# The projection of the token batches in two nested levels of seven products

## The chip, the cores and the metric

The kernel runs on one core of a Trainium2 chip. The metric is the time of one execution on the device in microseconds; before the change it is 779.3 us, the median of three runs (778.61 to 779.39).

## What is computed

Eight batches of 512 tokens (8 heads of 64) attend to 32 state rows for each head, and the state rows attend to the tokens. The two results, 8 x (512 + 32) = 4352 rows of 512 numbers, then go through a gated feed-forward layer, all in float32:

```python
scores = scale * np.matmul(x, state.transpose(0, 1, 3, 2))     # softmax over the state -> a
xread = np.matmul(a, state)
scores2 = scale * np.matmul(state, x.transpose(0, 1, 3, 2))    # softmax over the tokens -> a2
sread = np.matmul(a2, x)
attn = np.concatenate([xread, sread], axis=2)
# (batch, rows, heads * 64) -> x: 4352 x 512
xn = x / np.sqrt(np.mean(x * x, axis=-1, keepdims=True) + 1e-6) * rms_g
g = xn @ w_gate                                                # 512 x 1536
out = (g * (1.0 / (1.0 + np.exp(-g))) * (xn @ w_val)) @ w_out  # 1536 x 512
```

## The kernel before, in words

A batch of tokens has three kinds of work. Its *attention* (`tokens_read`, `states_read`) gives softmax weights `aT_s` and the state rows' results. Its *hidden* part (`hidden_seven`) gives `hb`, 1536 hidden channels by 512 tokens, held as 12 blocks of 128 channels. Its *projection* (`project_seven`) multiplies `hb` by `w_out`, held as `wo` in SBUF. The weights for the hidden part are first multiplied by the batch's own state rows (`own_weights`, L548, two blocks of 128 channels at a time), from `w_m`, which is fetched from DRAM for each batch in six pieces of 1 MB (`fetch`, L169). The state rows of all batches come last, as a stage of their own with half as many columns.

Hidden part and projection use the same trick: a product of two matrices, each cut into 2 x 2 blocks, is made from seven block products instead of eight, with sums of blocks before and after (Winograd's form of Strassen's method). In the projection, `hb` is cut into halves of its channels and of its tokens, `wo` into halves of its channels and of its columns. Each of the seven products of a batch is 2 x 6 matmuls with 128 x 128 stationary and 128 x 256 moving numbers. The sums of `wo` (`weight_sums`, three in `wt`, one in place of a block of `wo`) are made once; the sums of `hb` (`hs`, L908) are made by VectorE in each batch. Products that belong to more than one result accumulate in one PSUM bank: ScalarE copies a bank out (L893) before the next product is added to it, and VectorE adds other banks to the copies (L901), which are then stored (L923). There are two PSUM banks `fx` and one each of `fy` and `fz` for these sums, in the hidden part and in the projection alike.

In the hidden part of batches 1 to 7, VectorE adds the banks (L756), ScalarE takes tanh of half of the gate channels (L747), VectorE makes the gate from it (L759) and multiplies by the values (L771). L775 and L781 are two more sums of halves that the projection needs. GpSimd makes the sums of the own weights (L574 to L577) and of the softmax weights (`slot_sums`, L612 to L615).

For batches 2 to 7, tokens are transposed in 32 x 32 blocks by VectorE (L310), written to DRAM (`x_d`, L313) and read back (`xG`, L318) so that L328 can multiply them by the state; softmax weights go the same way (`e_d`, L475 and L479). These transfers are issued by ScalarE, all others by SyncE (SP). `x` of a batch comes as 16 transfers (L114) into one of two buffers.

The order of instructions on TensorE, VectorE and ScalarE is written out by hand as strings, one letter for one step of a stream: `ORDER` for batch 0 with the conversion of the weights, `PERIOD` for each of batches 1 to 7, `STATES` for the state rows. In `PERIOD`, `h`, `t`, `u` are products, copies and sums of the hidden part, `p`, `c`, `k` those of the projection, `v` and `x` products and copies of the own weights, and `a`, `s`, `w` the attention and first own weights of the next batch. GpSimd's and SP's instructions are not bound by the strings; the framework places them.

```python
    by_hand = dict(engines={mybir.EngineType.PE, mybir.EngineType.DVE,
                            mybir.EngineType.Activation})
...
        with tc.manual_schedule(**by_hand):
            for stream in PERIOD:
                if stream in streams:
                    step = next(streams[stream], done)
```

## Time and profile before

| quantity | value |
|---|---|
| median of three runs | 779.3 us |
| span of the profiled execution | 776.3 us |
| period of one batch, 2 to 6 | 83.48 us |
| TensorE busy in such a period | 83.5 us |
| VectorE, ScalarE, GpSimd busy in it | 57.3, 31.1, 21.7 us |
| data moved in it | 140 GB/s |
| states' hidden part (L694, 128 columns) | 717.94 to 753.67 us |
| granted TensorE clock | 1.000 |

The span runs from the first to the last instruction of one profiled execution; the median lies 3.0 us above it, and what lies around the span is not in the profile. A batch's period is the distance between the starts of its L328 matmuls. Busy time of TensorE is modelled by the profile: weight loads (PEld) overlap matmuls, and a float32 matmul appears as two instructions. A group's idle time is the time for which its engine stood still just before it.

### The profile page before, as it was taken

To read this page: it belongs to the slowest core of one execution; us is meant where nothing else is said; L and a number is where in the kernel's file an instruction comes from. 1 tells how busy PE (TensorE), PEld (TensorE's weight loads), DVE (VectorE), ACT (ScalarE), POOL (GpSimd) and SP (SyncE) were. 2 spreads that over 40 slices of the span, in tenths; PEclk is the share of its full clock that TensorE was granted. 3 is DMA by queue.
4 is the path that set the end of the run, shared out by engine and by line. 5 is a ranking of instruction groups with operands and counts; after the bars stand their busy time and mean duration, and the time that the engine had idled before them with its cause. 6 is when DMAs were issued, how large, how long until landed. Compare 5 with 4: busy or idle time off the path is not lost.

```text
span 776.3 us, 12116 instructions
## 1 busy us (share of the span) xinstructions
PE 764.7 (98%) x4726; PEld 586.1 (75%) x4726; DVE 538.0 (69%) x846; ACT 328.0 (42%) x538; POOL 162.8 (21%) x232
## 2 busy tenths in 40 slices
PE   6999999999999999999999999999999999999998
PEld 5643444788878887878878877888778878888996
DVE  4999988678647872888368764787378735881461
ACT  6798874554145222543245314532354314510320
POOL 2000004430053105320433015400621044300000
PEclk9999999999999999999999999999999999999999
DMA  9977845770266225630565036612543154100311
GB/s 291 258 261 284 320 148 159 200 260 4 92 196 255 59 72 184 237 109 35 160 211 196 1 102 223 243 34 69 204 163 109 42 174 165 55 14 27 124 55 28
DMA packets 73689, 113.00 MB, mean 146 GB/s; under 512 B 40864, under 2 KB 51616, under 8 KB 66720
## 3 DMA queue, kind: packets, MB, share of 16 engines
q1 hardware_dynamic: 60512, 92.75, 35.5%
q10 hardware_dynamic: 13120, 19.47, 8.5%
q8 instruction: 38, 0.62, 0.3%
q14 instruction: 19, 0.16, 0.1%
HBM read 87.56 MB, written 24.64 MB: 145 GB/s over the span
## 4 chain that ended last, share of the span: by engine, by line
PE 96%; DVE 2%; DMA 0%; POOL 0%; ACT 0%; issue 0%; SPq 0%
PE f L694 38%; PE f L856 36%; PE f L796 5%; PE pv L590 5%; PE at L548 3%; PE pv L548 3%; PE at L328 1%; PE at L490 1%; PE at L421 1%; PE at L300 1%; PE at L278 1%; DMA rows<-in_state_dram 0%; DVE raw L245 0%; DVE w_m L254 0%; DVE ex L249 0%; POOL ri L271 0%
## 5 line engine op out<-in xcount | busy, mean ns | idle before, releaser
L856 PE MATMUL f<-wo,hb 128*128 128x256 f32 x540 | 123.0, 382 | 0.0
L694 PE MATMUL f<-aT_s,v 128*128 128x256 f32 x504 | 119.7, 382 | 0.0
L856 PEld LDWEIGHTS f<-wo,hb 128*128 128x128 f32 x540 | 101.4, 190 | 23.2 <-issue 5.0
L694 PEld LDWEIGHTS f<-aT_s,v 128*128 128x128 f32 x504 | 93.5, 190 | 25.0 <-DVE c L756 5.9
L756 DVE TENSOR_TENSOR g<-g,f 128x512 f32<-128x512 f32 (+1 forms) x96 | 61.3, 650 | 68.3 <-PE f L694 40.3
L694 PE MATMUL f<-aT_t,vs 128*128 128x256 f32 x336 | 87.0, 381 | 0.0
L747 ACT ACTIVATE hb<-g 128x1024 f32<-128x1024 f32 (+1 forms) x48 | 48.3, 1005 | 87.6 <-DVE g L756 87.6
L271 POOL TENSOR_TENSOR ri<-ss,mhalf 128x4 f32<-128x4 f32 x8 | 9.1, 1132 | 349.6 <-DVE ss L375 233.5
L856 PE MATMUL f<-wt,hs 128*128 128x256 f32 x360 | 80.4, 379 | 0.0
L893 ACT COPY ot<-f 128x256 f32<-128x256 f32 x60 | 20.1, 371 | 134.7 <-PE f L856 134.7
L856 PEld LDWEIGHTS f<-wt,hs 128*128 128x128 f32 x360 | 68.2, 190 | 9.4 <-issue 0.2
L694 PEld LDWEIGHTS f<-aT_t,vs 128*128 128x128 f32 x336 | 63.2, 190 | 14.1 <-issue 5.0
L759 DVE SCALAR_TENSOR_TENSOR hb<-hb,g 128x1024 f32<-128x1024 f32 x42 | 53.8, 1281 | 13.1 <-ACT hb L747 13.1
L574 POOL TENSOR_TENSOR vs<-v 128x256 f32<-128x256 f32 x42 | 30.7, 731 | 137.5 <-ACT v L559 137.5
L559 ACT COPY v<-pv 128x512 f32<-128x512 f32 x42 | 22.7, 594 | 71.2 <-PE pv L548 71.2
L745 ACT COPY g<-f 128x512 f32<-128x512 f32 (+1 forms) x48 | 26.9, 560 | 56.3 <-PE f L694 56.3
L796 PE MATMUL f<-wo,hb 128*128 128x512 f32 x96 | 44.7, 598 | 0.0
L590 PE MATMUL pv<-aT_s,v 128*128 128x512 f32 x96 | 44.2, 597 | 0.0
L694 PE MATMUL f<-aT_s,vs 128*128 128x256 f32 x168 | 43.1, 379 | 0.0
L694 PE MATMUL f<-aT_t,v 128*128 128x256 f32 x168 | 43.1, 379 | 0.0
L856 PE MATMUL f<-wo,hs 128*128 128x256 f32 x180 | 41.5, 382 | 0.0
L856 PE MATMUL f<-wt,hb 128*128 128x256 f32 x180 | 40.8, 382 | 0.0
(142 smaller groups left out, 1245.0 us busy)
## 6 DMA issues: line engine op xcount, KB each, us to landing
w_m<-w_d SPq DMA_DIRECT2D x48, 1024.0 KB, 5.6
out_dram<-ot SPq DMA_DIRECT2D x56, 128.0 KB, 1.8
raw<-in_moe_w_val_dram SPq DMA_DIRECT2D x6, 1024.0 KB, 5.3
raw<-in_moe_w_out_dram SPq DMA_DIRECT2D x6, 1024.0 KB, 7.6
w_d<-w_m SPq DMA_DIRECT2D x6, 1024.0 KB, 4.9
x_b<-in_x_dram SPq DMA_DIRECT2D x96, 64.0 KB, 2.3
x_d<-xB ACTq DMA_DIRECT2D x6, 1024.0 KB, 4.3
xG<-x_d ACTq DMA_DIRECT2D x24, 256.0 KB, 5.0
```

What stands on the lines that cost most here:

```text
L548: TE.matmul(out=pv[e][Ns * j:Ns * j + Ns, :], lhsT=stT_g[b][D * e:D * e + D, j, :], rhs=w[D * e:D * e + D, j].rearrange("p m k f -> p (m k ...
L559: SE.copy(v[:, e].rearrange("p m k f -> p (m k f)"), pv[e])
L574: GE.tensor_tensor(out=vs[:, 0], in0=a21, in1=a22, op=ALU.add)
L590: TE.matmul(out=to[0], lhsT=lhs(i, k), rhs=r, start=(i == 0), stop=(i == len(rhs) - 1))
L694: TE.matmul(out=ps[:, i, 0:half], lhsT=l[:, i, :], rhs=r, start=(start and i == 0 and k == 0), stop=(k == len(lhs) - 1), skip_group_check= ...
L745: SE.copy(gates(q)[1], q["x"][:, :, 0:half])
L747: SE.activation(out=hb[:, 2 * mp:2 * mp + 2, 0:n].rearrange("p m (c t) -> p m c t", c=2), in_=q["g"][:, :, :, 0:half], func=ACTF.Silu if s ...
L756: VE.tensor_tensor(out=to, in0=to, in1=q[ps][:, :, 0:half], op=ALU.add)
L759: VE.scalar_tensor_tensor(out=h, in0=h, scalar=1.0, op0=ALU.add, op1=ALU.mult, in1=q["g"].rearrange("p m c t -> p m (c t)"))
L796: TE.matmul(out=banks[r], lhsT=hb[:, m, P * r:P * r + P], rhs=wo[:, m, :], start=(m == 0), stop=(m == NM - 1))
L856: TE.matmul(out=banks[name][:, r, :], lhsT=lhs(k)[:, P * r:P * r + P], rhs=rhs(k), start=(start and r == 0 and k == 0), stop=(k == HM - 1) ...
L893: SE.copy(to, banks[name][:, r, :])
```

## The change

In batches 1 to 7, the projection is done by `project_twice`: each of the seven products of half matrices is itself made from seven products of quarter blocks, so a batch has 49 products of 3 matmuls with 128 x 128 moving numbers. Batch 0 and the state rows are projected as before.

- The stationary side needs sums of quarters of `hb` or of its half sums: `quarter_sums`, four VectorE subtractions or additions of 384 elements a partition for each of the seven outer products, in two buffers.
- The moving side needs sums of quarters of `wo` and `wt`: `weight_quarters` makes them once, on GpSimd, during batch 1, three for each outer product, and writes them to DRAM; a fourth replaces a quarter in place. `fetch_quarters` reads the three (128 x 1152 numbers) for each outer product of each batch, into three buffers. `weights_back` undoes the sums in place, on GpSimd, ahead of the state rows.
- An outer product adds into two banks, of four and three quarters. ScalarE copies, VectorE adds banks, and `combine`, four GpSimd additions, makes the result from the seven quarters. The copies live in the two buffers that also hold `g` of the hidden part, and in one more.
- The gate of batches 1 to 7 is the activation function Silu itself instead of tanh with a VectorE step (L759 goes).
- `x` has one buffer after batch 0 and comes as four transfers of 256 KB; the token order that follows from this is put right by the store. `sS` has one buffer, `e2T` shares the one of `e2`.
- `PERIOD` is new, and the strings now also fix the order of GpSimd's and SP's instructions: fetches of weights (`f`), of quarter sums (`g`), loads (`l`) and stores (`o`) are streams of their own. In it L328 moves from the projection into the hidden part.

The diff, cut to its core:

```diff
-    "hhvthttxhauhhxhuauaahhtutaahtahvxvtuhuxxhuuhthtxuthuhtuhhuhuhhutuhutthuxuhxtxuhh"
-    "vhuuthhxthxtahuhathuuuxuuauthuthtahhuthuuuhuhpuuuhtuuucauapaaasaspkacpaspsspaaaa"
-    "aaaapkkcpccaakaaascuskaappkaaaaapssssaaaaksapkakasswwwxxpxkxxpccssx"
+    "vxqqhthtfhthhaxhhqqquuttuxahhhththhhuuuauutthqhaaaaGthutuvqqxxvxxqxhuhhqxutuhhtu"
+    "haukkthtvxqxxhhhhhuaaauutttkhhukqqqquuuathhhhhafaauutttsqauhhhhuthqqGuuusuqqqGgp"
+    "upauhqqfqstuuupgppukpppppaakplpfckkkkpqakaaqqgaakkqgkcppppppppppkakkkkoakkppapsc"
+    "cpkpcpggacakpsopakaappakpsakppksaaakkksppppppgkakakppakaakaookkakssppsosppcofasa"
+    "wwxxxssspcwxxxloof"
...
-        x_sb[b] = two.tile([P, NC, H * D], F32, name="x_b")
-        if b > 1:
-            for i in range(4 * NC):
-                c, g = divmod(i, 4)
-                nc.sync.dma_start(
-                    out=x_sb[b][Ns * g:Ns * g + Ns, c].rearrange("p (h d) -> p h d", h=H),
-                    in_=x[b, :, P * g + Ns * c:P * g + Ns * c + Ns, :].rearrange("h p d -> p h d"))
-            return
+        x_sb[b] = (one if b else x_0).tile([P, NC, H * D], F32, name="x_b")
...
-        sS = read[b] = two.tile([P, 2, NC, P], F32, name="sS")
+        sS = read[b] = (one if b else x_0).tile([P, 2, NC, P], F32, name="sS")
...
-        e2T = one.tile([P, 4, 2, NC, Ns], F32, name="e2T")
+        e2T = e2
...
+        if b == 1:
+            load_state(2)
+            load_x(2)
...
-            fetch(b * (NM // 2) + mp + W_BUFS)
+            if b == 0 or b == 1 and mp < 2:
+                fetch(b * (NM // 2) + mp + W_BUFS)
...
-        seven["pool"] = ctx.enter_context(tc.tile_pool(name="halves", bufs=7))
+        seven["w2"] = ctx.enter_context(tc.tile_pool(name="quarters_w", bufs=3))
+        seven["s2"] = ctx.enter_context(tc.tile_pool(name="quarters_h", bufs=2))
+        seven["k"] = ctx.enter_context(tc.tile_pool(name="kept", bufs=1))
...
+    def fetch_quarters(n):
+        if n < 7 * (B - 1):
+            w2_sb[n] = seven["w2"].tile([P, 3, QM, QD], F32, name="w2")
+            nc.sync.dma_start(out=w2_sb[n], in_=t2_d[n % 7])
+    def weight_quarters():
+        for o, (b11, b21, b12, b22) in enumerate(map(by_columns, outer_weights())):
+            w2 = seven["w2"].tile([P, 3, QM, QD], F32, name="w2")
+            for to, a, b in ((w2[:, 0], b12, b11), (w2[:, 1], b22, w2[:, 0]),
+                             (w2[:, 2], b21, w2[:, 1]), (b12, b22, b12)):
+                GE.tensor_tensor(out=to, in0=a, in1=b, op=ALU.subtract)
+                if to is b12:
+                    nc.sync.dma_start(out=t2_d[o], in_=w2)
+                yield
+    def by_columns(r):
+        return [r[:, QM * i:QM * i + QM, QD * j:QD * j + QD] for j in range(2) for i in range(2)]
...
+    def project_twice(b, store):
+        first = 7 * (b - 1)
+        hs = seven["s"]
+        def A(i, j):
+            return hb[:, HM * j:HM * j + HM, HS * i:HS * i + HS]
+        lefts = [A(0, 0), A(0, 1), A(0, 0), hs, A(1, 0), A(0, 1), A(1, 1)]
+        banks, inner, kept = {}, {}, {}
+        def bank(name, fresh):
+            if fresh:
+                pools = (fx, fx) if name == "x" else (fy, fz)
+                banks[name] = [pools[i].tile([P, 4 - i, QD], F32, name="f") for i in range(2)]
+            return banks[name]
+        def products():
+            rights = outer_weights()
+            for o in range(7):
+                name, fresh = "xyxzxzx"[o], o in (0, 1, 3)
+                to = bank(name, fresh)
+                (a11, a12, a21, a22), (b11, b21, b12, b22) = quarters(lefts[o]), by_columns(rights[o])
+                for n, (half, slot, lhs, rhs) in enumerate((
+                        (0, 0, a11, b11), (0, 2, a12, b21), (0, 3, a22, 2), (0, 1, 1, 1),
+                        (1, 2, 0, 0), (1, 1, 2, b12), (1, 0, 3, b22))):
+                    if isinstance(lhs, int):
+                        lhs = inner[o][:, lhs]
+                    if isinstance(rhs, int):
+                        rhs = w2_sb[first + o][:, rhs]
+                    for k in range(QM):
+                        TE.matmul(out=to[half][:, slot, :], lhsT=lhs[:, k, :], rhs=rhs[:, k, :],
+                                  start=(fresh and n in (0, 4) and k == 0), stop=(k == QM - 1),
+                                  skip_group_check=True)
+                    yield
+        def copies():
+            for what, name, pool in (("p1", "x", "g"), ("u2", "x", "g"), ("p5", "z", "k"), ("c21", "x", "g")):
+                k = kept[what] = (two if pool == "g" else seven["k"]).tile(
+                    [P, 8, QD], F32, name="kept", tag="g" if pool == "g" else "kept")
+                for i in range(2):
+                    SE.copy(k[:, 4 * i:4 * i + 4 - i], banks[name][i])
+                    if what == "c21" and i:
+                        combine(what, 1, 0)
+                    yield
+        ready = {}
+        def stores():
+            for what in ("p1", "p5", "u2", "c21"):
+                for r in range(2):
+                    store(*ready[what][r])
+                    yield
+        def combine(what, i, j):
+            k = kept[what]
+            ready[what] = []
+            GE.tensor_tensor(out=k[:, 1:3], in0=k[:, 0:1].to_broadcast([P, 2, QD]), in1=k[:, 1:3],
+                             op=ALU.add)
+            GE.tensor_tensor(out=k[:, 5:8:2], in0=k[:, 1:2].to_broadcast([P, 2, QD]),
+                             in1=k[:, 5:7], op=ALU.add)
+            GE.tensor_tensor(out=k[:, 1], in0=k[:, 5], in1=k[:, 6], op=ALU.add)
+            GE.tensor_tensor(out=k[:, 0:4:3], in0=k[:, 5:8:2], in1=k[:, 3:5], op=ALU.add)
+            for r in range(2):
+                at = 2 - 2 * r
+                ready[what].append((2 * i + r, HD * j, HD, k[:, at:at + 2].rearrange("p c f -> p (c f)")))
+        def add(what, name, i, j):
+            k = kept[what]
+            for n in range(2):
+                part = k[:, 4 * n:4 * n + 4 - n]
+                VE.tensor_tensor(out=part, in0=part, in1=banks[name][n], op=ALU.add)
+                if n:
+                    combine(what, i, j)
+                yield
+        def quarter_sums(o):
+            a11, a12, a21, a22 = quarters(lefts[o])
+            s = inner[o] = seven["s2"].tile([P, 4, QM, QD], F32, name="h2")
+            VE.tensor_tensor(out=s[:, 0], in0=a21, in1=a22, op=ALU.add)
+            yield
+            VE.tensor_tensor(out=s[:, 1], in0=s[:, 0], in1=a11, op=ALU.subtract)
+            yield
+            VE.tensor_tensor(out=s[:, 2], in0=a11, in1=a21, op=ALU.subtract)
+            yield
+            VE.tensor_tensor(out=s[:, 3], in0=a12, in1=s[:, 1], op=ALU.subtract)
+            yield
+        def half_sums(to, a, b):
+            for k in range(0, HM, QM):
+                VE.tensor_tensor(out=to[:, k:k + QM], in0=a[:, k:k + QM], in1=b[:, k:k + QM],
+                                 op=ALU.subtract)
+                yield
+        def sums():
+            yield from quarter_sums(0)
+            yield from quarter_sums(1)
+            yield from half_sums(A(0, 0), hs, A(0, 0))
+            yield from quarter_sums(2)
+            yield from add("p1", "y", 0, 0)
+            yield from half_sums(A(0, 1), A(0, 1), A(0, 0))
+            yield from quarter_sums(3)
+            yield from quarter_sums(4)
+            yield from quarter_sums(5)
+            yield from add("p5", "x", 1, 1)
+            yield from quarter_sums(6)
+            yield from add("u2", "z", 0, 1)
+        return products(), copies(), sums(), stores()
...
+            rows_ = out[T * b:T * b + S, c0:c0 + n]
+            if b < 2:
+                rows_ = rows_[P * r:P * r + P]
+            else:
+                rows_ = rows_.rearrange("(c g t) n -> g c t n", g=4, t=Ns)[r]
...
-                            mybir.EngineType.Activation})
+                            mybir.EngineType.Activation, mybir.EngineType.Pool,
+                            mybir.EngineType.SP})
...
-        h, t, u = hidden_seven(S, weights_of(b), lambda b=b: tokens_of(b), False)
-        p, c, k = project_seven(S, store_tokens(b))
...
+            h, t, u = hidden_seven(S, weights_of(b), lambda b=b: tokens_of(b), True)
+            p, c, k, o = project_twice(b, store_tokens(b))
+            streams.update(o=o, f=fetches(b), g=fetches_of_quarters(b))
+            if b == 1:
+                streams.update(q=weight_quarters(), G=first_fetches_of_quarters())
+            if b + 1 < B:
+                streams.update(l=loads(b + 2) if b + 2 < B else iter((0, 0)), a=tokens_read(b + 1), s=states_read(b + 1),
+                               w=first_products(b + 1, then))
```

## The prediction

> **What bounds the kernel now.** I read the page's busy shares first, then its chain of waits, then the chain in order of time for one batch, then the stretch table for the same batch.
>
> ```profile
> span 776.3 us, 12116 instructions
> ...
> PE 764.7 (98%) x4726; PEld 586.1 (75%) x4726; DVE 538.0 (69%) x846; ACT 328.0 (42%) x538; POOL 162.8 (21%) x232
> ...
> PE 96%; DVE 2%; DMA 0%; POOL 0%; ACT 0%; issue 0%; SPq 0%
> ```
>
> TensorE is 96% of the chain that ends last. A batch repeats every 83.48 us (the matmuls of L328 start at 263.99, 347.47 and 430.94), and inside it TensorE never rests; VectorE does for a third of the time:
>
> ```profile
> 347.47:430.94 83.47, 83.47 (x544) 66.91 (x550) 57.27 (x94) 31.06 (x56) 21.63 (x29) 1.00 0.43 140
> ```
>
> (time, then busy us and instructions of PE, weight load, DVE, ACT, POOL; clock; DMA share; GB/s). So an instruction less on TensorE is time saved, as long as nobody makes it wait. The chain, batch by batch, gives the projection (L856) and the only place where 128-column matmuls run in a row, the states' stage:
>
> ```profile
> 260.54 2.59 PE f L856 x12
> 263.13 0.86 PE f L694 x4
> 263.99 1.02 PE at L328 x16
> 265.01 18.33 PE f L856 x84
> 284.38 7.97 PE f L856 x36
> 292.48 2.69 PE f L856 x12
> ...
> 298.51 5.38 PE f L856 x24
> ...
> 717.94 35.73 PE f L694 x320
> ```
>
> A float32 matmul in the code is two instructions here. The five pieces of L856 are 168 instructions, 36.96 us. In uninterrupted runs (2.59 for 12) one of 256 columns takes 0.2158 us; the 0.70 us above 168 of those is lost at changes to other shapes. One of 128 columns takes 35.73 / 320 = 0.1117 us, weight load included.
>
> **What the Trainium skill says.** "TensorE: Matmul & The Clock Gate", Back-to-back issue gap, gives N/2.4 + 2.5 ns a pass, and "FP8 and Floating Point Precision", TensorE Precision Notes, four passes for true float32, so two per instruction: 111.7 ns at 128 columns, 218 at 256. The trace agrees (111.7; 216). "SBUF — State Buffer", SBUF: two separate sides, says that GpSimd and a VectorE instruction with two SBUF inputs share one port pair and block each other. The trace agrees: the subtraction L781 takes 0.69 us alone and 1.10 beside GpSimd, whose sum then takes 1.18 instead of 0.73.
>
> ```profile
> 502.47 1.18 POOL L576 TENSOR_TENSOR v<-v 128x256 f32<-128x256 f32 x1
> ...
> 503.10 1.10 DVE L781 TENSOR_TENSOR hb<-hb 128x512 f32<-128x512 f32 x1
> ...
> 509.70 0.69 DVE L781 TENSOR_TENSOR hb<-hb 128x512 f32<-128x512 f32 x1
> ```
>
> "ScalarE: Activation LUTs", What ACT_TABLE_LOAD costs: 1283 ns; the trace shows 1.28.
>
> **The change, part by part.**
>
> *TensorE.* Per batch, 84 matmuls of 256 columns become 49 x 3 = 147 of 128: 294 instructions for 168 (the built program lists 1029 of them for seven batches, so the change does what it says). 168 x 0.2158 = 36.26 us becomes 294 x 0.1117 = 32.83; the 0.70 at changes of shape stays. Saving 3.43 us a batch, 24.0 in seven. The arithmetic falls by an eighth, but the fixed part of each instruction doubles.
>
> *VectorE.* Out: L759 (6 x 1.27), L908 (4 x 0.94), L901 (6 x 0.41) = 13.8 us. In: 28 quarter sums of 384 elements, not in this trace; rows that follow each other start 0.60 us apart at 512 elements and 0.91 at 768, so 0.47 (bounds: 0.47, and 0.83 if each ran at L781's contended rate). 28 x 0.47 = 13.2; four half sums 3.6; six adds of 512 or 384 elements 3.2. About +6 us, 63 of 80: it fits by total. But 24 quarter sums lie in the projection, with the half sums, the adds and 13.6 us of the next batch's attention (L397 to L434, as before): 31.7 us beside 37.5 of TensorE (32.8 plus the L421, L490, L548 and other matmuls put between). I walked the order of both engines from the first quarter product. An outer product lasts 7 x 0.67 = 4.69 us, and its fourth inner product needs its second quarter sum. Only two buffers hold such sums, so VectorE can't run ahead by more than one product.
>  - First product: its second bank is freed by the last gate of the hidden part, due at 3.05 us after that start; TensorE wants it at 3.56. Fits.
>  - Fourth product (start 14.95, needs the sum at 16.96): VectorE ends its sums for the third at 11.75, then adds (13.2), half sums (15.0), sum, attention piece, sum: 16.6. The slack of 0.4 goes to GpSimd: the combine of the first result begins at 13.2 on just these instructions, four of them at +0.27 to +0.41 (L775 and L781 beside GpSimd). Late by 0.7 to 1.2; TensorE's own changes of shape give some 0.3 back: 0.6 us.
>  - The L421 matmuls in the fifth wait for the second transpose of the attention: 0.2. The norm's chain in the seventh (sum, L370, L375, GpSimd's power, L278): 0.2.
>
> *GpSimd.* In: four combines of four, 256 wide (0.73, next start 0.69 later) or 128 (about 0.46): 2.6 us each, 10.4 a batch, to 32 of 80. The third stands ahead of the slot sums (L612) and the first sums of the next hidden part. They then end at 42.95, where TensorE wants the last of them at 42.9: 0.1.
>
> *ScalarE.* Silu for tanh has the same shape (1.06 us). Two table loads a batch, 2.6 us: one while it waits for the first gate of a batch, one before the exponentials, which wait for VectorE until 4.6 us into the projection (tanh and exp needed none). Nothing, with 49 us of idle ScalarE as cover; without it up to 1.3 each.
>
> *DMA.* In: 7 fetches of 576 KB a batch; 11.7 MB become 15.8, 140 to about 195 GB/s, where the trace reaches 426 in a 5 us stretch. Each is issued when the third buffer before it is freed, 9 us or more ahead of its use, and 1 MB lands in 5.6: nothing. SP's order is now fixed: behind the last store of a batch, which waits for GpSimd some 6 us into the hidden part, stand the next weights' two fetches; used 10 us later, 5.6 to 9.0 to land: nothing. x now has one buffer, so its loads (4 x 256 KB, 5.8 us each when together) start after L490 and have some 11 us before the first transpose (L310). The read-back xG is the tight one: before, its last issue stood 7.6 us ahead of L328 (506.7 to 514.4). Now three of four stand behind the copies of the last own product, with seven hidden products (7 x 0.876 = 6.1 us) to L328; landing took 2.9 to 5.5 after an issue spread of about 1 us. 0.2 us (bounds 0 to 2).
>
> *First and last batch.* Batch 1 also makes the quarter sums of the weights: 28 GpSimd instructions of 384 elements, about 1.0 us each by width, between its other sums; the hidden part has about 45 us for these 28 and the 16 or so others (12 us), and VectorE is slowed beside them: 0.7 more. Batch 7 has no next attention: 0.2 in all.
>
> *Sum.* 6 x 1.3 + 0.7 + 0.2 = 8.7 us of new waits against 24.0: -15.3. The profiled span of 776.3 becomes 761.0; the median lies 3.0 above that span and I keep this: 764.0.
>
> **The rivals.**
>  - *Nothing waits.* 779.3 - 24.0 = 755.3. For it: every fit above is within half a microsecond, and the order of before shows no idle TensorE at all. Against it: VectorE at 85% in the projection with two buffers. 0.25.
>  - *Transfers late.* The traffic that grew by a third and the single x push x, x_d and xG back so that L328 waits 2 us more in each of batches 1 to 6: 764 + 6 x 2 = 776. For it: a chain of three transfers with one buffer; against: no DMA stretch was full except one of 426 GB/s. 0.12, together with VectorE late by as much.
>  - *Slower: VectorE sets the pace of the projection.* Its 31.7 us grow by the port: three combines, power and slot sums, 17 GpSimd instructions, each blocking it for 0.41 to 0.69 us, 7 to 11.7. At the upper end 43.4 against 37.5: 5.9 of waiting, 2.5 more than is saved, 779.3 + 6 x 2.5 - 3.2 = 791. It decides once the average sum passes (37.5 + 3.4 - 31.7) / 28 + 0.47 = 0.80 us. For it: the measured 1.10 against 0.69. Against: only sums of two SBUF inputs block, and combines overlap a few of them. 0.11.
>
> **How the numbers follow.** Forecast case (waits of 0.7 to 2 us a batch, 759 to 769): 0.52; nothing waits: 0.25; transfers or VectorE late by 2 to 3.4 (769 to 779): 0.12; slower: 0.11. The range from 755 to 776 leaves out the slower case and the end of the third. A measurement tells 0.2% (1.6 us) from no change, so below 777.7 is faster: 0.52 + 0.25 + 0.09 = 0.86; same 0.03; slower 0.11.
>
> **What would show it.** The projection's instructions at 0.112 us and the batch's period at 81 to 82 us (before 83.48); idle of TensorE's weight loads released by the VectorE quarter sums, most in the fourth outer product; quarter sums near 0.54 us each, longer where a combine runs. Wrong: a period below 80.3 (no waits), a period over 83 with those sums over 0.8 us, or L328 waiting for xG by more than 1 us.

## The result, and the profile after

The changed kernel takes 799.05 us (median of four runs, 796.5 to 799.9), the kernel before 778.95 beside it on the same chip: a ratio of 1.0252, interval 1.0234 to 1.0271. It is slower by 2.5%; forecast was 764.0, with slower at a chance of 0.11, and for another reason than the one that came true.

The page of after, its span, its busy times and its chain of waits:

```profile
span 797.9 us, 14335 instructions
...
PE 759.2 (95%) x5608; PEld 603.8 (76%) x5608; DVE 611.0 (77%) x1000; ACT 351.8 (44%) x548; POOL 292.6 (37%) x379
...
PE 69%; DVE 20%; DMA 6%; POOL 2%; issue 2%; ACT 1%; SPq 1%; ACTq 0%; DVEq 0%; POOLq 0%
PE f L696 34%; PE f L998 11%; PE f L798 5%; PE pv L592 5%; DMA out_dram<-kept 4%; DVE hb L1057 3%; PE at L549 3%; PE f L1134 2%; PE f L861 2%; DVE kept L1038 2%; DVE h L1046 2%; DVE h L1048 2%; DVE h L1052 1%; DVE hb L771 1%; PE pv L549 1%
```

TensorE was 96% of the chain and is 69% now. The two newcomers are VectorE with 20% and, as the first line that is not arithmetic, a store (`out_dram<-kept`) with 4%. Line numbers are those of the changed kernel: L696 is the hidden part's product (L694 before), L998 the twofold projection (L856 before).

The stretch table for two batches, from the start of one projection to the start of the next (columns as in the prediction):

```profile
354.60:440.70 86.10, 82.47 (x664) 69.50 (x664) 65.94 (x117) 35.17 (x58) 34.43 (x45) 0.98 0.57 184
526.53:610.64 84.11, 80.77 (x664) 68.55 (x663) 66.25 (x116) 35.16 (x58) 34.88 (x45) 1.00 0.59 188
```

TensorE now rests 3.6 and 3.3 us in these stretches, and in the first its granted clock is below 1. These stretches, of both kernels and of the best version that the experiments led to (`e7_xg`, below), in us:

| stretch | before | after | `e7_xg` |
|---|---|---|---|
| start to batch 1's projection | 176.9 | 180.1 | 179.2 |
| from batch 1's projection to batch 2's | 83.5 | 88.6 | 87.9 |
| 2 to 3, 3 to 4, 4 to 5 | 83.5 each | 85.9, 86.1, 85.8 | 81.4, 81.5, 81.8 |
| 5 to 6, 6 to 7 | 83.5, 85.4 | 84.1, 86.4 | 82.6, 82.2 |
| batch 7's projection and the states | 96.7 | 100.9 | 94.8 |
| span | 776.3 | 797.9 | 771.4 |

So the loss is spread over all batches. Where it sits in one, the chain of waits in order of time shows, from the last sums of a projection to the next hidden part (L696):

```profile
389.24 1.15 DVE kept L1038 x2
...
390.88 0.74 POOL kept L1026
...
392.15 0.70 POOL kept L1029
...
392.87 0.54 SPq L1110
...
393.46 6.35 DMA out_dram<-kept
...
399.91 0.59 ACT g L742
...
400.64 4.52 PE f L696 x12
```

Read from below: TensorE waits for ScalarE's first copy of a gate (L742). That copy writes to one of the two buffers `g`, the one which holds u2, a quarter of the projection's result (the code calls the four quarters p1, u2, p5 and c21). It can be written only when u2's store has landed. VectorE finished u2 at 390.4, GpSimd combined it until 392.85, SyncE issued the store, and the store took 6.35 us. Before, such a store of 128 KB landed after 1.8 us (median of 56), and nothing of the hidden part waited for one:

```profile
out_dram<-ot SPq DMA_DIRECT2D x56, 128.0 KB, 1.8
```

The stop is on TensorE's timeline:

```profile
396.90 1.02 PE L696 MATMUL f<-aT_t,vs 128*128 128x256 f32 x4
400.64 1.69 PE L696 MATMUL f<-aT_t,vs 128*128 128x256 f32 x4 [2.71 <-ACT g L742]
402.12 1.91 PE L696 MATMUL f<-aT_s,vs 128*128 128x256 f32 x4
```

It is 2.71 us long. After it four instructions (two matmuls of the code) take 1.7 to 1.9 us instead of 1.03. The stretches of 2 us around it say why; the granted clock is the third value from the end:

```profile
398.00:400.00 2.00, 0.00 (x0) 0.00 (x0) 0.00 (x0) 0.09 (x1) 1.92 (x4) 1.00 0.97 289
400.00:402.00 2.00, 1.36 (x4) 1.19 (x5) 0.00 (x0) 0.98 (x2) 1.92 (x4) 0.75 0.65 188
402.00:404.00 2.00, 2.00 (x6) 1.53 (x6) 0.00 (x0) 1.62 (x3) 1.92 (x4) 0.50 0.71 158
```

The clock falls to a half 3.1 us after TensorE stopped, when it is already back, and stays there until 404.4 (the next stretch of 2 us has a mean of 0.89). Such stops stand at the start of the hidden parts of batches 3 to 7 and of the state rows: 2.59, 2.71, 2.51, 2.44, 2.60 and 2.74 us, 15.6 together. After five of the six the clock was at a half for 3.41 us. In batches 3 to 5 the 12 instructions after the stop took 4.40 to 4.52 us; in batch 6, after the stop of 2.44 us, the clock did not fall and they took 2.83. That is 1.6 us more each time, some 8 us together, and most of the difference between the two rows of the stretch table above.

The length of the stop is not what separates batch 6 from the others: in `e7_xg` the clock fell after a stop of 2.19 us. The five falls, at 315.69, 401.02, 486.35, 657.02 and 738.94, lie 25, 25, 50 and 24 steps of 3.413 us apart (those of `e3_warm` 26, 26 and 26). So the clock changes at fixed steps, wherever a stop begins; in batch 5 it fell 0.1 us before TensorE was back, in batch 3 it fell 1.1 us after. In the step before each fall TensorE rested 2.3 to 2.7 us. Batch 6's stop of 2.44 us was cut in two by the end of a step, and the step that held most of it had 1.86. The step before the fall in batch 5, and that one of batch 6 (TensorE's busy time is the second value):

```profile
482.94:486.35 3.41, 1.02 (x5) 0.57 (x3) 0.00 (x0) 0.60 (x2) 3.25 (x6) 1.00 0.87 289
568.27:571.69 3.42, 1.56 (x8) 1.03 (x6) 0.00 (x0) 0.54 (x2) 3.26 (x6) 1.00 1.02 338
```

Which of the six stops paid was thus a matter of where it lay.

### The profile page after: what moved, and what is told of

Its sections match the earlier page's. It is cut to its first block, busy times and chain, and to the rows that moved or that the text cites. A ratio compares the mean times of both kernels' runs of the same rounds, so it can differ in the third digit from the quotient of the medians.

```text
span 797.9 us, 14335 instructions
## 1 busy us (share of the span) xinstructions
PE 759.2 (95%) x5608; PEld 603.8 (76%) x5608; DVE 611.0 (77%) x1000; ACT 351.8 (44%) x548; POOL 292.6 (37%) x379
## 4 chain that ended last, share of the span: by engine, by line
PE 69%; DVE 20%; DMA 6%; POOL 2%; issue 2%; ACT 1%; SPq 1%; ACTq 0%; DVEq 0%; POOLq 0%
PE f L696 34%; PE f L998 11%; PE f L798 5%; PE pv L592 5%; DMA out_dram<-kept 4%; DVE hb L1057 3%; PE at L549 3%; PE f L1134 2%; PE f L861 2%; DVE kept L1038 2%; DVE h L1046 2%; DVE h L1048 2%; DVE h L1052 1%; DVE hb L771 1%; PE pv L549 1%
## 5 line engine op out<-in xcount | busy, mean ns | idle before, releaser
L696 PE MATMUL f<-aT_s,v 128*128 128x256 f32 x504 | 119.9, 385 | 0.0
L696 PEld LDWEIGHTS f<-aT_s,v 128*128 128x128 f32 x504 | 96.5, 194 | 19.4 <-issue 5.2
L696 PE MATMUL f<-aT_t,vs 128*128 128x256 f32 x336 | 88.6, 388 | 12.9 <-ACT g L742 12.9
L1024 POOL TENSOR_TENSOR kept<-kept 128x256 f32<-128x256 f32 x28 | 23.4, 835 | 200.2 <-DVE z L410 120.3
L1008 ACT COPY kept<-f 128x512 f32<-128x512 f32 (+1 forms) x56 | 29.7, 531 | 136.5 <-PE f L998 78.3
L998 PE MATMUL f<-w,h 128*128 128x128 f32 x588 | 75.5, 278 | 8.8 <-DVE h L1048 8.2
L696 PEld LDWEIGHTS f<-aT_t,vs 128*128 128x128 f32 x336 | 64.2, 193 | 23.7 <-POOL kept L1026 14.7
L998 PEld LDWEIGHTS f<-w,h 128*128 128x128 f32 x588 | 69.6, 192 | 15.5 <-DVE h L1048 10.0
L696 PE MATMUL f<-aT_s,vs 128*128 128x256 f32 x168 | 48.4, 414 | 0.0
L696 PEld LDWEIGHTS f<-aT_s,vs 128*128 128x128 f32 x168 | 32.2, 202 | 21.0 <-issue 10.1
L771 DVE TENSOR_TENSOR hb<-hb,f 128x512 f32<-128x512 f32 (+1 forms) x48 | 31.2, 649 | 19.7 <-PE f L696 19.4
L696 PE MATMUL f<-aT_t,v 128*128 128x256 f32 x168 | 43.6, 382 | 1.3 <-DVE c L758 1.3
L998 PE MATMUL f<-wo,h 128*128 128x128 f32 x336 | 42.3, 275 | 0.0
L998 PE MATMUL f<-wo,hb 128*128 128x128 f32 x336 | 42.1, 275 | 0.0
L771 DVE TENSOR_TENSOR hb<-hb,c 128x512 f32<-128x512 f32 (+1 forms) x48 | 38.0, 791 | 3.9 <-ACT hb L749 2.9
```

The costliest lines, as they stand in the source:

```text
L696: TE.matmul(out=ps[:, i, 0:half], lhsT=l[:, i, :], rhs=r, start=(start and i == 0 and k == 0), stop=(k == len(lhs) - 1), skip_group_check= ...
L771: VE.tensor_tensor(out=part, in0=part, in1=val, op=ALU.mult)
L998: TE.matmul(out=to[half][:, slot, :], lhsT=lhs[:, k, :], rhs=rhs[:, k, :], start=(fresh and n in (0, 4) and k == 0), stop=(k == QM - 1), s ...
L1008: SE.copy(k[:, 4 * i:4 * i + 4 - i], banks[name][i])
```

## The experiments

Ratios are to the kernel before, run on the same chip, with their 95% intervals. The runs were on several chips, on which the kernel before took 778.5 to 779.4 us, so differences between their times of less than 1 us say nothing.

| run | us | ratio | interval |
|---|---|---|---|
| after | 799.05 | 1.0252 | 1.0234 to 1.0271 |
| `e1_swap` | 785.35 | 1.0076 | 1.0061 to 1.0091 |
| `e2_actq` | 824.5 | 1.0592 | 1.0558 to 1.0627 |
| `e3_warm` | 811.32 | 1.0416 | 1.0391 to 1.0442 |
| `e4_swap_nop1` | 778.07 | 0.9985 | 0.9957 to 1.0014 |
| `e5_c21` | 778.55 | 1.0004 | 0.9993 to 1.0016 |
| `e6_sums` | 776.46 | 0.9967 | 0.9959 to 0.9975 |
| `e7_xg` | 772.99 | 0.9929 | 0.9914 to 0.9944 |
| `e8_nox` | 801.72 | 1.0307 | 1.0277 to 1.0337 |
| `e9_plain` | 775.55 | 0.9959 | 0.9944 to 0.9974 |
| `e10_now2` | 807.58 | 1.0368 | 1.0341 to 1.0395 |
| `e11_defer` | 787.19 | 1.0096 | 1.0073 to 1.0120 |
| `e12_noq` | 772.18 | 0.9908 | 0.9889 to 0.9926 |
| `e13_split` | 807.89 | 1.0357 | 1.0328 to 1.0386 |
| `e14_x16` | 787.72 | 1.0103 | 1.0070 to 1.0136 |
| `e15_all` | 778.38 | 0.9995 | 0.9982 to 1.0009 |
| `k2` | 836.14 | 1.0732 | 1.0705 to 1.0759 |
| `k8` | 781.24 | 1.0040 | 1.0028 to 1.0051 |
| `k16` | 778.60 | 0.9991 | 0.9983 to 1.0000 |

The theory from the two traces: u2's store holds back the next hidden part, and the clock falls after that stop. The rival is the one of the prediction: VectorE and the port that it shares with GpSimd set the pace of the projection.

### Is it the buffer? (`e1_swap`, `e5_c21`)

```diff
-            for what, name, pool in (("p1", "x", "g"), ("u2", "x", "g"), ("p5", "z", "k"), ("c21", "x", "g")):
+            for what, name, pool in (("p1", "x", "g"), ("u2", "x", "k"), ("p5", "z", "g"), ("c21", "x", "g")):
```

> The changed kernel with two buffers exchanged: the copy of u2 goes into the buffer of its own (k), the copy of p5, which is stored earlier, into one of the two buffers shared with the gate. Theory (the first gate copy of the next hidden part waits for the store of u2, and TensorE's clock falls after that stop): the stops of 2.4 to 2.7 us at the start of the hidden parts of batches 3 to 7 and of the state rows go, 15.9 us together, and with them the stretches at half clock, 1.7 us in five of them, 8.6 us: 799 - 24.5 = 774.5, period of a batch 81.6, granted clock 1.00. Rival (VectorE and the shared port set the pace of the projection, and TensorE would only wait for them instead): the period stays above 83.5 and the time above 786.

Measured 785.35: of the six stops at a first gate copy none is left that is longer than 0.32 us, but 11 us of the expected gain are missing. The time alone is only just below the rival's 786; what speaks against the rival is that TensorE did not wait for VectorE in place of the stops (its waits for quarter sums, L1048, are 9.0 us in all, 8.2 in the changed kernel). The profile of `e1_swap` has two successors. In batch 7 the second gate copy waits for the last store, c21's:

```profile
650.86 2.04 PE L696 MATMUL f<-aT_t,vs 128*128 128x256 f32 x4 [3.32 <-ACT g L742]
```

The clock was at a half for 6.83 us there, which costs some 3.4 us more. In other batches ScalarE stands before the issue of a read of `xG` (L319), which waits until the write of `x_d` has landed, and the copy L745 behind it on ScalarE is what TensorE waits for (0.7 to 1.6 us in three batches):

```profile
333.51 0.31 ACTq L319 DMA_DIRECT2D xG<-x_d  x1
333.86 0.58 ACT L745 COPY c<-f 128x512 f32<-128x512 f32 x1 [3.51 <-DMA x_d<-xB]
```

These three, 3.3, 3.4 and 3.6 us, are 10 of the 11 us. In the changed kernel the first stop and its half clock, 4.3 us together, had left both transfers the time to land. `e5_c21` removes the first of them:

```diff
+                if pool == "h2":
+                    k = seven["s2"].tile([P, 4, QM, QD], F32, name="h2").rearrange(
+                        "p a k t -> p (a k) t")[:, 0:8]
```

> The kernel with exchanged buffers, and the copy of c21 in a buffer of the quarter sums that is free by then, so that no gate copy waits for a store of the projection. With u2's wait gone, the trace of the exchanged buffers shows the next of the kind: in batch 7 the second gate copy waits 4.2 us for c21's stores (TensorE 3.3 us, and half clock after it), in other batches up to 0.8. Theory: 785.35 - 3.3 - 1.7 = 780.3. Rival (another wait takes the place at once, as c21's did): 783 or more.

Measured 778.55, so no equal wait took its place (own weights wait 0.5 to 1.8 us for their fetch in three batches of the profiled execution, which with 782.28 was the slowest of the 20). With no copy in a buffer that the next part needs soon, all of the 20 us are gone, and the kernel is at the time of the one before.

### Why does the store land late? (`e2_actq`, `e8_nox`, `e10_now2`, `e9_plain`)

```diff
-                    store(*ready[what][r])
+                    store(*ready[what][r], nc.scalar if what == "u2" else nc.sync)
```

> The changed kernel with the two stores of u2 issued by ScalarE instead of SyncE, the buffers as they were. If the store takes 6.2 us to land because it stands in SyncE's queue between the fetches of quarter sums, the stores of p5 and the fetches of weights and x, it lands in about 2 us here, before TensorE needs the bank: time as with the exchanged buffers, 774 to 776. If it is slow because the DMA engines are full at that time, whichever queue it comes from, it still takes 5 us or more and the time stays at 794 to 799.

Measured 824.5, outside both expectations: u2's stores, issued at 397.63 and 398.30, let the gate copy go only at 408.36, and the stops of batches 3 to 7 grew to 5.7 to 6.1 us. So a store that stands outside SyncE's queue doesn't land earlier; why it landed later still was not tried.

```diff
+        if b > 2:
+            x_sb[b] = x_kept[0]
+            return
```

> The changed kernel, which reads x for batches 0, 1 and 2 only; later batches use batch 2's x again, so the loads of x (L120, 256 KB each in pieces of 256 bytes) at the end of the periods are left out. If these loads fill the DMA engines and SyncE's queue, and so make u2's store land after 6.2 us and hold back c21's store by 9: u2's store lands in 3.5 us or less, no stop in the later batches, no half clock, 773 to 779. If the store is slow by itself or because of the weight fetch of 1 MB, it still lands after 5 us or more, and the time stays above 790.

Measured 801.72: the stops stay at 2.3 to 3.3 us without any load of `x`. The theory that these loads fill the queue falls.

```diff
+        if 14 <= n < 7 * (B - 1):
+            w2_sb[n] = w2_sb[n - 3]
```

> The changed kernel without the fetches of quarter sums (576 KB each, L944) from batch 3 on; later batches use the last three that were fetched. If the two or three of them that stand ahead of u2's store in SyncE's queue make it land late: 3.5 us or less, no stop from batch 4's hidden part on, about 780. If the row pattern of the store is the cause, it stays near 5 us and the time above 790.

Measured 807.58. The store ahead of the stop landed after 4.67 us, the stop fell to 1.1 us: the fetches account for some 1.5 of 6.2 us, not for the rest. The time rose all the same, because L329 now waited for `xG`, 9.0 us in seven places; why, was not tried.

```diff
-            if b < 2:
-                rows_ = rows_[P * r:P * r + P]
-            else:
-                rows_ = rows_.rearrange("(c g t) n -> g c t n", g=4, t=Ns)[r]
+            rows_ = rows_[P * r:P * r + P]
```

> The changed kernel with the stores of batches 2 to 7 to 128 rows that follow each other, as batches 0 and 1 store (the rows of the output then stand in the order of the four large x transfers, which is not put right). In the kernel before such a store of 128 KB landed after 1.8 us and took 0.33 us to issue; in the changed one it takes 0.54 us to issue and lands after about 5 us, in the run without x loads too. If the row pattern (4 x 32 rows of 1 KB) is what makes it slow: u2's store lands in 2 to 3 us, no stop at the start of a hidden part, no half clock, c21's store early enough as well: 776 to 781. If the transfers beside it make it slow, it still lands after 4.5 us or more and the time stays above 790.

Measured 775.55: this one line is worth 23.5 us. No hidden part waits for a store by more than 0.42 us, and the clock is 0.999. So the loss comes from the form of the store, which the four large transfers of `x` make necessary. The form is not the whole of the landing time: a plain store of this kernel lands after 4.0 us (median of 56), one of the kernel before after 1.8. That is just soon enough here.

### What is slow in that form? (`e13_split`, `k2`, `k8`, `k16`)

```diff
+            for c in range(4):
+                t0 = P * c + Ns * r
+                nc.sync.dma_start(out=rows_[t0:t0 + Ns], in_=ot[Ns * c:Ns * c + Ns])
```

> The changed kernel with each store of batches 2 to 7 cut into four of 32 rows (32 KB), to the same rows of the output as before. With rows that follow each other the stops went (775.6). If the pattern of one transfer over 4 x 32 rows is what makes a store land late, four transfers of 32 rows each land in 2 to 3 us, and the time is 775 to 780, unless their 32 issues a batch of about 0.33 us instead of 8 of 0.54 us crowd SyncE (6 us more a batch). If it is the addresses of the rows themselves (every fourth group of 32 rows), they land after 4.5 us or more still, and the time stays above 790.

Measured 807.89. The last of the 16 stores of p5 and u2 landed 1.55 us after its issue, but SyncE needed 7.90 us for the 16 issues, so it came no earlier:

```profile
391.85 7.90 SPq L1111 DMA_DIRECT2D out_dram<-kept  x16
```

The landing speaks for the pattern of one transfer and against its addresses, though each transfer moves only a quarter of the bytes; the time can't, since SyncE took the place. "DMA: Bandwidth & Descriptors", Why a DMA increments its semaphore by 16 and not by 1, of the Trainium skill names a mechanism: a transfer runs on k of 16 DMA engines, the largest k that divides the slowest dimension of both patterns. Rows "c t" with four values of c would then use 4 engines, and a plain store of 128 rows 16. The last three runs change that number alone:

```diff
-                rows_ = rows_.rearrange("(c g t) n -> g c t n", g=4, t=Ns)[r]
+                rows_ = rows_.rearrange("(c g t) n -> g c t n", g=4, t=64)[r]   # k2; 16 in k8, 8 in k16
```

> The changed kernel with each store of batches 2 to 7 as one transfer to 2 groups of 64 rows, 256 rows apart, instead of 4 groups of 32 (the rows of the output are then not in their right order). Theory: a store runs on as many of the 16 DMA engines as its outermost count of groups allows; with 2 each engine moves 64 KB instead of 32, so u2's store lands after about 9 us instead of 6.2, the stops grow by about 3 us in six places: 799 + 18 = 817, and more where the clock falls. Rival (what counts is that rows of four results interleave in the output, or the length of a group): longer groups land as fast or faster than 32 rows, 799 or less.

> The same with 8 groups of 16 rows. Theory (8 engines, 16 KB each): u2's store lands in about 4 us, at most a short stop at the start of a hidden part, clock 1.00: 778 to 784. Rival: shorter groups that interleave more land no faster than 4 x 32 rows, 797 or more.

> The same with 16 groups of 8 rows. Theory (16 engines, 8 KB each, as a store to rows that follow each other): no stop, the time of the plain store, 775.6 within 2 us, though the rows of four results interleave in every group of 32. Rival (interleaving): 797 or more.

The chain of `k2` at the place that the first fence of after's chain shows, and then that of `k8`:

```profile
398.26 10.89 DMA out_dram<-kept
```

```profile
388.32 3.98 DMA out_dram<-kept
...
392.40 0.59 ACT g L742
...
393.13 2.83 PE f L696 x12
```

Landing takes 10.6 to 10.9 us with 2 groups, 6.1 to 6.35 with 4 (batches 3 to 7), 3.9 to 4.1 with 8 (batches 3 to 6). With 16 the store is no part of the chain until batch 7, where it takes 2.40 (2.90 in `k8`); u2's stores of batches 3 to 6 land after 3.3 to 4.0 us. So the landing falls from 2 to 4 to 8 groups, and from 8 to 16 hardly any more. The times are 836, 799, 781 and 779. In `k8` the 12 instructions after the stop (0.3 to 0.6 us in batches 3 to 6) take 2.83 us, so the clock holds there. Shorter groups interleave more and land faster: the rival falls. The engines themselves are not in these profiles, so that each group count stands for a number of engines is the page's word; that the landing shortens with the number of groups is shown from 2 to 8, and what sets the 4 us that remain is not. `k16` is 3 us above the plain store, where its expectation allowed 2; `k2` is 19 us above its expectation, with stops of 6.1 to 8.1 us.

### What does the half clock cost by itself? (`e3_warm`)

```diff
+                if warm and mp == 0:
+                    q["y"] = fy.tile([P, 2, HS], F32, name="f")
+                    for i in range(11):
+                        TE.matmul(out=q["y"][:, 0, 0:P], lhsT=ident, rhs=ident, start=True, ...
```

> The changed kernel with eleven 128 x 128 matmuls of the identity (2.46 us of TensorE) put where TensorE stops at the start of the hidden parts of batches 3 to 7 and of the state rows, into a bank that is free there; the wait for the store of u2 stays. They fill the stop and add nothing to it. If the half clock after the stop is a cost of its own: clock 1.00, 12 matmuls after the stop in 2.8 us instead of 4.5, 1.7 us less in five places: 799 - 8.6 = 790.4. If the slow matmuls have another cause (operands that come late), the time stays at 799 or rises.

Measured 811.32. TensorE's timeline in `e3_warm`:

```profile
311.93 2.62 PE L725 MATMUL f<-ident 128*128 128x128 f32 x22
314.38 1.04 PE L696 MATMUL f<-aT_t,vs 128*128 128x256 f32 x4
...
324.35 0.89 PE L696 MATMUL f<-aT_t,vs 128*128 128x256 f32 x3 [3.63 <-ACT g L748]
```

The filled stop keeps the clock: the four instructions after it take 1.04 us. But the next pair's gate copy then stood 3.63 us for c21's store, and the clock fell there. The first stop had covered the second. So the run gives no total for the half clock; its price is read from the changed kernel itself, 3.41 us at half the clock five times, which is 1.7 us of lost work each (1.6 by the 12 instructions).

### The projection: port and VectorE (`e4_swap_nop1`, `e6_sums`, `e11_defer`)

`e4_swap_nop1` is `e1_swap` without GpSimd's four additions for p1:

```diff
-                    combine(what, i, j)
+                    combine(what, i, j, what != "p1")
```

> The kernel with exchanged buffers, without GpSimd's four additions that make p1 from its quarters (p1's quarters are stored uncombined). If these additions, on the port that VectorE shares, cause the wait before the fourth outer product: that wait falls from 0.9 to 0.2 us in each of seven batches, time 774.5 - 5 = 769.6. If VectorE is late there by its own work, the wait stays and the time is that of the exchanged buffers within 1 us.

Measured 778.07, 7.3 us less than `e1_swap`. The timeline of after at this place has the additions and the half sums (L1057) side by side, and the stop behind them:

```profile
367.96 2.35 DVE L1057 TENSOR_TENSOR hb<-hb 128x768 f32<-128x768 f32 x2
...
368.19 1.30 POOL L1026 TENSOR_TENSOR kept<-kept 128x256 f32<-128x256 f32 x1
...
370.23 0.81 DVE L1046 TENSOR_TENSOR h<-hs 128x384 f32<-128x384 f32 x1
...
370.96 1.21 DVE L413 TENSOR_TENSOR eS<-eS,z 128x512 f32<-128x512 f32 x1
372.09 0.55 DVE L1048 TENSOR_TENSOR h<-h,hs 128x384 f32<-128x384 f32 x1
...
372.69 0.38 PE L998 MATMUL f<-w,h 128*128 128x128 f32 x1 [0.91 <-DVE h L1048]
```

Without them, in `e4_swap_nop1`, the same VectorE instructions are short, and TensorE doesn't stop:

```profile
362.31 1.81 DVE L1058 TENSOR_TENSOR hb<-hb 128x768 f32<-128x768 f32 x2
...
364.04 0.55 DVE L1047 TENSOR_TENSOR h<-hs 128x384 f32<-128x384 f32 x1
...
364.51 0.68 DVE L413 TENSOR_TENSOR eS<-eS,z 128x512 f32<-128x512 f32 x1
```

GpSimd's additions are the cause of this stop, by the port that the two share, as the prediction had it: over the half sums, the sum and L413 VectorE is late by 1.3 us. `e6_sums` (on `e5_c21`) tried the order on VectorE instead:

```diff
-            yield from half_sums(A(0, 1), A(0, 1), A(0, 0))
             yield from quarter_sums(3)
+            yield from half_sums(A(0, 1), A(0, 1), A(0, 0))
```

> As the run before in this call, and the two half sums that the sixth outer product needs are moved behind the quarter sums of the fourth. They stood ahead of them on VectorE, 1.2 us and more beside GpSimd's additions. If VectorE's order there causes the wait of 0.9 us before the fourth outer product, it goes in seven batches: 780.3 - 6 = 774. If the wait is GpSimd's alone, or is shifted to the fifth or sixth product, 779 or more.

Measured 776.46. The stop before the fourth product is gone, and the L422 matmuls in the fifth take 2.05 us a batch instead of 1.04: it has been shifted, not removed, as the rival said, though not at the rival's 779. The 2 us gained are not this stop's; where they come from was not settled. `e11_defer` moved p1's additions behind p5's:

```diff
-                if n:
+                if n and what != "p1":
                     combine(what, i, j)
+                if n and what == "p5":
+                    combine("p1", 0, 0)
```

> The kernel with buffers separated, half sums moved and xG issued by SyncE (773.0), and GpSimd's additions for p1 moved behind those for p5, its stores with them. They then run 12 us later, where VectorE has more slack. Without them the kernel with exchanged buffers was 7.3 us faster. Theory: 1.0 us in each of six batches, 773.0 - 6 = 767. Rival: they slow VectorE as much at the new place, in the sixth and seventh product: 772 or more.

Measured 787.19. No product waits for a sum there except in batches 1 and 7, but four own weights (L549) wait 1.15 to 3.36 us for their fetch (`w_m`): with p1's stores moved, SyncE's queue has another order. That this order is what makes the fetch late is likely, and was not tried.

### ScalarE's queue and batch 1 (`e7_xg`, `e12_noq`)

```diff
-                nc.scalar.dma_start(
+                nc.sync.dma_start(
                     out=xT[Ns * q:Ns * q + Ns]...
```

This is `e6_sums` with the read of `xG` moved.

> As the run before in this call, and the four reads of xG are issued by SyncE instead of ScalarE. With exchanged buffers ScalarE stood 3.5 us before such an issue (the write of x_d took 10.6 us to land), and behind it the copy that TensorE waited for, 0.7 to 1.6 us in three batches. Theory: these go, 774 - 3.6 = 770.4, with L329 still on time. Rival: SyncE now stands there, the third fetch of weights behind it, and own weights or L329 come late: 774 or more.

Measured 772.99, 0.71% faster than the kernel before and the fastest with the whole computation. No L745 waits for `x_d` any more. A stretch of it:

```profile
348.50:430.00 81.50, 81.50 (x663) 68.31 (x663) 66.04 (x117) 35.28 (x58) 34.04 (x45) 1.00 0.61 194
```

`e12_noq` is `e7_xg` with 7 of the 28 subtractions that make the weights' quarter sums:

```diff
-                GE.tensor_tensor(out=to, in0=a, in1=b, op=ALU.subtract)
+                if a is b12:
+                    GE.tensor_tensor(out=to, in0=a, in1=b, op=ALU.subtract)
```

> The same kernel without the move of p1, and with only 7 of the 28 GpSimd subtractions of batch 1 that make the quarter sums of the weights (the other 21 are left out, the one sum is written to all three places). The period of batch 1 is 87.9 us there against 81.4 to 82.6 for the next ones. If these subtractions, on VectorE's port, cost that: 83 to 84, time 773.0 - 5 - 1 = 767. If batch 1 is long for another reason (its own attention, first fetches), the time stays at 772 or more.

Measured 772.18. Batch 1's stretch fell from 87.9 to 85.2, while its start moved from 179.2 to 180.4. In `e7_xg` TensorE rested 4.2 us in this stretch, all of it for VectorE; the longest stop, 2.19 us before L422, was followed by 3.41 us at half the clock. In `e12_noq` no such wait is left, and VectorE's instructions of the stretch take 66.5 us instead of 71.0. But L491 waited 2.15 us for a transfer (`e_d`), and again 3.41 us at half the clock followed:

```profile
218.88 1.25 PE L491 MATMUL at<-x_b,e 128*32 128x64 f32 x64 [2.15 <-DMA e<-e_d]
```

This stop and about 1.7 us of half clock are the whole difference between 85.2 and the 81.5 of the next stretches. So the subtractions' share in batch 1 is some 4 us of waits, and another stop took most of the gain away. Why that transfer was late was not tried; this kernel also writes each product's sums in three transfers instead of one.

### Undoing the large x transfers (`e14_x16`, `e15_all`)

```diff
+        if b > 1:
+            for i in range(4 * NC):
+                ...
-                rows_ = rows_.rearrange("(c g t) n -> g c t n", g=4, t=Ns)[r]
+                rows_ = rows_[P * r:P * r + P]
```

> The changed kernel with one part undone: x comes in 16 transfers of 64 KB in the old token order, so the stores are to rows that follow each other, and the order of the output is that of the kernel before; x keeps its one buffer. If the large x transfers cost the 20 us by the store pattern that they need: 775 to 778, as with the plain store. If it is the single buffer of x, whose load now stands between the stores, whatever its form: above 785.

Measured 787.72, between the two. The stops at the start of the hidden parts are gone and the clock is 1.000. In their place own weights wait for their fetch by 0.9 to 2.0 us in four batches, which stands behind 16 issues of `x`:

```profile
396.02 11.10 SPq L122 DMA_DIRECT2D x_b<-in_x_dram  x16
407.22 2.07 SPq L1113 DMA_DIRECT2D out_dram<-kept  x2
409.39 5.23 SPq L177 DMA_DIRECT2D w_m<-w_d  x3
```

With one buffer, all of `x` has to come in the few us between its last use and its next, and SyncE's time is what is short: 11.10 us here, 8.18 to 9.05 with four transfers. Before, 14 of the 16 stood in a row as well (6.89 us), but went into a second buffer, and no own weights waited. That SyncE's time is the cause is argued from this order; it was not tried by itself.

> The kernel with buffers separated, half sums moved and xG issued by SyncE (773.0), and with x in 16 transfers and plain stores as in the run before in this call. In 773.0 no store made TensorE wait any more. If stores were the only cost of the large x transfers: 772 to 774. If plain stores also speed the weight fetches and xG behind them: 768 to 771. If 16 transfers put SyncE late: 776 or more.

Measured 778.38 (773.3 to 784.3 in 20 of 22 runs, 785.8 and 786.7 in the other two): no better than `e7_xg`, where stores already made no one wait, and more uneven.

## Why the prediction was wrong, step by step

- *TensorE.* Right. Twelve instructions of 128 columns take 1.34 us (0.1117 each), and the stretch of `e7_xg` without waits for sums, 81.50, is 83.48 less 1.98 with 1.0 of waiting for L422 and some changes of shape in it.
- *VectorE, fourth product.* The mechanism was right: GpSimd's additions for p1, on the half sums and the sum behind them. The size was 0.91 us a batch instead of 0.6, and 1.12 and 1.32 in two products of batch 7. Quarter sums take 0.55 us and follow each other at 0.47, as estimated, and up to 1.37 beside GpSimd.
- *DMA: "nothing".* This step failed. It costed the fetches that were added, and took the stores for what they were. It said that the fetches of weights stand behind the last store and that this costs nothing; it never asked who waits for the stores. Two of them now hold buffers of `g` that the next hidden part writes, so they were on the path: between the end of u2's combine (392.85) and the time at which TensorE would have needed the copy done (397.9, less 0.7 for the copy) there were 4.3 us, and issue and landing took 6.9. In place of "nothing" stand 15.6 us of stops, and some 8 of half clock after them, as the runs without slow stores confirm together (`e9_plain` 23.5 less, `e5_c21` 20.5).
- *"The token order that follows from this is put right by the store".* The section on the change says this, and the prediction gives it no price. It cut the store to 4 groups of rows, which land after 6.2 us, where plain stores of the same kernel land after 4.0 and those before after 1.8. That only four groups were left could be read from the pattern in the diff.
- *x and xG.* L329 was not late (no wait for `xG` in after), so the bound of 2 us was not needed. The late transfer acted elsewhere: ScalarE stood before the issue of L319, with a copy behind it, 0.7 to 1.6 us in three batches of `e1_swap`. The prediction named the queue, and not what is queued behind.
- *Batch 1: 0.7.* Too small. Its stretch is 88.6, and still 87.9 in `e7_xg`, where 80.05 plus 2.0 were forecast. TensorE rests 4.8 us of the 88.6, 4.2 of them for VectorE, which GpSimd's subtractions slow; without most of these (`e12_noq`) no such wait is left.
- *GpSimd, ScalarE.* GpSimd is busy for 34.4 to 34.9 us in a batch where 32 were forecast. Silu's two table loads a batch stand behind no stop of TensorE, as forecast.
- *The rivals.* "VectorE sets the pace" gave the right sign for a wrong reason: without slow stores the same VectorE work gives 775.6. "Nothing waits" lies 18 us below the best version.

Of the 35 us between forecast and result, stops and half clock are 23.5, batch 1 and the stretch before it some 10 (3.2 + 88.6 - 82.05); the remaining 2 are the fourth product and those of batch 7.

## What to carry to other kernels

When a buffer gets a second use, follow the buffer to its last reader: if that is a store, the store's landing is on the path of the next writer, and the landing has to be costed with the pattern it will have, not with that of the stores before. Here the pattern alone moved the landing of the same 128 KB between 10.6 us (2 groups of rows) and about 4 (8 groups or more), and cutting each store into four transfers moved the price to the queue that issues them. After a stop is removed, look for the ones that it covered: here three stood behind it.

## What the runs showed of the hardware

- One store of 128 KB in rows of 1 KB: 10.6 us to land over 2 groups of rows, 6.2 over 4, 3.9 over 8 and 3.3 to 4.0 over 16, in kernels that differ in nothing else.
- TensorE's clock fell to a half for 3.41 us after five stops of 2.51 us and more, and not after one of 2.44 us. "TensorE: Matmul & The Clock Gate", What's actually happening, gives a window of 3.4 us that runs freely. The trace agrees with that: the falls lie whole multiples of 3.413 us apart. But a window need not be all rest: those before the falls had 2.3 to 2.7 us of it. So a stop shorter than the window can be charged for, depending on where it lies, and the charge falls on the work after it. How much rest is enough is not settled: in batch 1 of `k8` the clock fell after a stop of 1.04 us.
- SyncE needs about 2 us to issue a transfer of 256 KB in pieces of 256 bytes (8.18 us for four), 0.7 us for a quarter of it.
